# Chunks 3 to 7 of a DeltaNet and PReLU block: the first pair by seven products too, odd steps with keys ahead of rows

## The chip, the cores and the metric

The kernel runs on one core of a Trainium2 chip. The time of a run is the device time of that core in microseconds; less is better. Engines are named as the profile names them: PE is TensorE (PEld its loads of weights), DVE is VectorE, ACT is ScalarE, POOL is GpSimd, SP is SyncE, whose queue issues nearly all transfers.

## The reference

Two blocks run one after the other. The first is DeltaNet attention (4 batches, 8 heads, 768 tokens, head dimension 48), a recurrence over a 48 x 48 state for each head. The second turns its output into 3072 rows of 384 numbers and sends them through two matrices with a PReLU between them. Everything is 32-bit floating point.

```
k_n = k / (norm(k) + 1e-6);  state = 0
for t in range(768):                                    # for each batch and head
    y[t]  = q[t] @ state
    v_old = k_n[t] @ state
    state = state + beta[t] * outer(k_n[t], v[t] - v_old)
x = y as (3072, 384)
h = x @ w_in                                            # w_in: 384 x 2048
g = max(h, 0) + alpha * min(h, 0)                       # alpha: one slope per column
out = g @ w_out                                         # w_out: 2048 x 384
```

## The kernel before

**Steps and chunks.** The sequence is cut into 12 chunks of 64 tokens. A step is one chunk for two of the four batches (`steps`, L115), so step n belongs to chunk n // 2, and there are 24. The attention of a step is solved by blocks: keys and queries are transposed on PE (`flips`, L478), Gram products of the keys are made nine steps ahead (`grams`, L513), a triangular system is inverted for four steps at once on DVE (`eliminate`, L588: 30 multiplications and additions at L602 and L608, and transposes at L577), and the state is used and updated (`through_state`, L838, `solve`, L951, `outputs`, L963, `next_state`, L977).

**The feed-forward part.** Once both steps of a chunk are through, their 256 rows go through the two matrices. `to_ffn` (L999) transposes the outputs y of a step on PE (L1006), and ACT copies them from PSUM into the tile `xt` of the chunk (L1010). The 2048 columns of the first matrix are 8 pairs of 128-column blocks. A *plain* pair (`plain`, L1316) is six matmuls of 128 x 256 (L1321), a Relu on ACT (L1326) and two operations on DVE (L1328). In chunks 3 to 11 most pairs are instead done by a scheme of seven products over four quarter blocks (`pair`, L1335): four *shared* products of 128 columns into a bank of PSUM (`common`, L1370, matmul at L1357), which ACT copies out (L1376) and POOL combines by three additions (L1381), and three *own* ones (`own`, L1359, matmuls at L1347 and L1352), with the third block of 128 rows done plainly. Its *total* is one DVE operation (L1385), then come a Relu on ACT (L1391), in chunks 3 to 7 two scalings on ACT (L1394), and the *slope*, one operation on DVE (L1398). The scheme needs sums of blocks of `w_in`, which POOL makes once (`input_sums`, L1257), and sums of blocks of `xt`, which DVE makes for each chunk (`token_sums`, L1292, four operations at L1303). The second matrix follows in seven products (`ffn_out_faster`, L1456, matmuls at L1481, additions at L1477).

**Pairs before the change.** In chunks 3 to 7 pairs 1 to 6 (`QUICK`, L1228) are done by seven products and pairs 0 and 7 are plain (L1431 and L1438); from chunk 8 on all eight are by seven products.

**PSUM.** From step 8 on there are two double tiles `p_pair` for attention and four banks for the feed-forward part, two named `p_ffn` and two `p_more`. The two double tiles are handed out in turn (`ps_big`, L78). A bank can be written again when its last reader is done.

**Order.** The order on each engine is written out by hand: engines run their instructions in program order. The feed-forward part is a generator (`feed_forward`, L2061) that yields 76 parts a chunk, 48 for the first matrix and 28 for the second, and `weave` (L1529) deals its parts between the other work. A step n from 8 on has three stretches (loop at L2102). First `burst_a(n)` (L1575): outputs and state update of step n - 1, then the state product of step n. Then `turn_round(n)` (L1617): the rows of step n - 1 and the flips of later keys and queries. Then `burst_b(n)` (L1601): the solve of step n, Gram products, queries and products for the steps after. `FILL` and `FILLS` (L2099, L2100) say how many parts of the feed-forward part go into each of the three stretches, and `TURNS` and `PIECES_OF` (L2098, L2094) how many pieces of the elimination go with them. What a burst leaves for later (`later`) is spread over the stretch. Within the first matrix, `Due` (L1271) issues a pair's total, Relu and slope so many parts after its start.

Of the kernel before, what the change touches and what calls it, by code (L numbers as in the profile page):

```python
# [25 lines left out]
FP32 = mybir.dt.float32  # L26
# [13 lines left out]
ASK = 8  # L40
# [5 lines left out]
def kernel(  # L46
# [340 lines left out]
        two("a_t", [128, H, C]), two("r", [128, 2, G, D]), two("u", [128, 2, G, D])  # L387
    )

    def one_of(tiles, n):  # L390
        return tiles[n % 2 if n < ONE else 0]

# [26 lines left out]
        stats[n] = (first_norm[:, n], first_weight[:, n])  # L419

    def squared(n):
        ksq[n] = work.tile([128, H, D], FP32, name="ksq", bufs=2)
        nc.scalar.square(ksq[n], early(n)[:, :, 0:D])

    def norms(n):
# [11 lines left out]
    def weigh(n):  # L437
        if n >= N:
            return []
        norm = stats[n]  # L440
        root(norm)
        return [lambda: weigh_rest(n, norm)]
# [782 lines left out]
        yield  # L1225

    held = {}
    QUICK = range(1, FP - 1)  # L1228
    beyond_sums = sums[:, FP // 2 : FP]
    late_pads = [x.rearrange("p h d -> p (h d)") for x in (k_late[0], masks_[1])]  # L1230

    def spare(x):

        if not held:
            held["same"] = work.tile([128, NJ, H, HB], FP32, name="same", bufs=1)
        return held["same"].rearrange("p j h c -> p (j h c)")[:, x * 256 : x * 256 + 256]

    def units_of(tile_):
        names = " ".join("abc"[: len(tile_.shape) - 1])
        return tile_.rearrange(f"p {names} -> p ({names})").rearrange("p (i e) -> p i e", e=128)  # L1240

    def group_sums(which, x):

        if which == 0:
            return units_of((k_early[0], k_early[2], q_pad[1])[x])
        if which == 3:
            return spare(x).rearrange("p (i e) -> p i e", e=128)
        return units_of((rights_, solved_)[which - 1][1])[:, x : x + 1]

    GROUPS = [slice(1, 5), slice(5, 6), slice(6, 7), slice(0, FP, FP - 1)]  # L1250

    def input_sum(x, i):

        which = 3 if i in (0, FP - 1) else max(i - 4, 0)
        return group_sums(which, x)[:, i - 1 if which == 0 else i // 7]

    def input_sums(which):  # L1257

# [48 lines left out]
    def ffn_in_fast(c):  # L1307
# [103 lines left out]
        def run(gen):  # L1411
            for _ in gen:
                due.step()
                yield

        if some:
            for at in (44, 47, 55, 60):
                due.put(at, lambda: next(first, None))
            for at in (52, 53, 57, 62):
                due.put(at, lambda: next(rest, None))  # L1420
            own_banks = [ffn_banks[(BANK + i) % 3] for i in (0, 1)]
            q_banks, three_z = [ffn_banks[3], ffn_banks[(BANK + 2) % 3]], [sums[:, 0 : FP // 2, 2], *two_z]
            pairs = {
                i: pair(i, own_banks[i % 2], q_banks[i % 2], three_z[i % 3]) for i in QUICK
            }
            for i, (_, _, total, below, slope) in pairs.items():
                late = i - (FP - 2)
                due.put(PER * i + (9 if late < 0 else 7), total)
                due.put(PER * i + {0: 10, -1: 12}.get(late, 13), below)
                due.put(PER * i + {0: 12, -1: 16}.get(late, 17), slope)  # L1430
            yield from plain(0, own_banks[0])  # L1431
            for i in QUICK:
                if i == QUICK[0]:
                    yield from run(pairs[i][1]())
                if i + 1 in QUICK:
                    yield from run(pairs[i + 1][1]())
                yield from run(pairs[i][0]())
            yield from plain(FP - 1, q_banks[(FP - 1) % 2])  # L1438
            return

        due.put(PER * 6 + 5, lambda: next(first, None))
# [14 lines left out]
    def ffn_out_faster(c):  # L1456
# [53 lines left out]
        if last:  # L1510
            store(c, 0, o[0], left)
        yield from some(p[6], sum_(2), weight(1, 1), range(FP - 2))
        if c + 1 < NCH:
            assert c + 1 in whole
            token_sums(c + 1)
        yield from some(p[6], sum_(2), weight(1, 1), range(FP - 2, FP))
        add(o[0][:, right_], o[0][:, right_], p[6])
        store(c, 0, o[0], right_ if last else slice(0, DM))
# [97 lines left out]

    def turn_round(n):  # L1617

        if n > JOINED:
            to_ffn(n - 1)  # L1620
        flips(n + EARLY + 1, n + 2)
        later = weigh(n + EARLY + 1)
        load_next(n)
        load_q(n + 3)
        return later
# [434 lines left out]

    def feed_forward():  # L2061
        yield from ffn_in(2)
        for which in range(3):
            input_sums(which)
        for i, _ in enumerate(ffn_out_fast(2)):
            if i == FAST_PARTS - 2:
                assert SOME in whole
                token_sums(SOME)
            yield
        for c in range(SOME, NCH):  # L2070
            yield from ffn_in_fast(c)
            if c == ALL - 1:
                input_sums(3)
            yield from ffn_out_faster(c)

    tail = feed_forward()
# [8 lines left out]
    for n in range(NJ, JOINED):  # L2085
# [95 lines left out]
```

## Time and profile before

| | |
|---|---|
| median of 3 runs | 646.55 us (646.39 to 647.15) |
| the profiled execution | 646.92 us |
| span of its profile | 645.2 us |
| busy, PE / DVE / ACT / POOL | 628.4 / 502.8 / 300.0 / 192.3 us |
| start of the plain pair 0 of chunks 3 to 7 | 219.15, 270.41, 320.31, 371.07 and 419.43 us |
| granted TensorE clock | 0.996 of full speed |

The span is what the profiler sees between the first and the last instruction; the run's time is 1.7 us longer. In the page and in the answers of the trace, a group of instructions is given with its line in the kernel, its engine, operation, tiles and shape. A matmul of 32-bit numbers is recorded as two instructions, so x12 stands for six. Matmuls overlap, so the time of one is read from the distance between the starts of its neighbours and not from its own length. "Idle before" names what an engine last waited for.

### The profile page before, as it was taken

What the parts mean: (1) busy time and instruction counts of PE and PEld (TensorE: products, weight loads), DVE (VectorE), ACT (ScalarE), POOL (GpSimd) and SP (SyncE); (2) the same over time, 40 slices, a digit from 0 to 9 for tenths busy, and PEclk for the clock granted to TensorE, in tenths of its full rate; (3) what the DMA queues carried; (4) which work ended last, traced back from release to release, by engine and by line L of the source; (5) the groups of instructions that cost most, each with busy time, mean ns of one, the idle gap of its engine ahead of it and who ended that gap; (6) DMA issues with size and microseconds to landing.
All of it is one profiled execution on the core that took longest, in us unless ns stands there. A gap on an engine that the chain in (4) does not pass through costs nothing.

```text
span 645.2 us, 22078 instructions
## 1 busy us (share of the span) xinstructions
PE 628.4 (97%) x9357; PEld 561.9 (87%) x9357; DVE 502.8 (78%) x1182; ACT 300.0 (47%) x695; POOL 192.3 (30%) x358
## 2 busy tenths in 40 slices
PE   7899999999999989999999999999999999999997
PEld 6687777566889989999989989999999999999997
DVE  5868789978997889868969958969968478377383
ACT  6676654254553276177177267057055054041230
POOL 7267610010161051052041043044053053062350
PEclk9989999999999999999999999999999999999999
DMA  7756864113301311311312111111211210100000
GB/s 130 202 157 174 240 150 117 28 24 69 71 18 24 76 33 20 70 30 28 60 30 39 35 40 28 36 42 26 46 34 25 54 24 1 42 11 2 26 1 24
DMA packets 106802, 36.92 MB, mean 57 GB/s; under 512 B 99872, under 2 KB 103088, under 8 KB 106704
## 3 DMA queue, kind: packets, MB, share of 16 engines
q1 hardware_dynamic: 104832, 35.03, 24.6%
q8 instruction: 73, 1.20, 0.8%
q10 hardware_dynamic: 1872, 0.49, 0.4%
q14 instruction: 25, 0.20, 0.1%
HBM read 30.78 MB, written 4.72 MB: 55 GB/s over the span
## 4 chain that ended last, share of the span: by engine, by line
PE 77%; DVE 12%; ACT 4%; DMA 3%; issue 2%; POOL 1%; SPq 0%; DVEq 0%; POOLq 0%; ACTq 0%
PE p_more L1481 15%; PE p_ffn L1481 11%; PE p_more L1357 5%; PE p_ffn L1155 5%; PE p_ffn L1347 4%; PE p_more L1347 3%; PE p_ffn L1112 3%; PE p_ffn L1352 3%; PE p_ffn L1177 3%; PE p_more L1352 3%; PE p_pair L784 2%; PE p_pair L467 2%; PE p_ffn L1321 2%; PE p_more L1321 2%; PE p_pair L844 2%
## 5 line engine op out<-in xcount | busy, mean ns | idle before, releaser
L1381 POOL TENSOR_TENSOR sums<-sums 128x128 f32<-128x128 f32 x186 | 109.7, 593 | 206.0 <-ACT sums L1376 196.3
L1112 PE MATMUL p_ffn<-xt,w_in 128*128 128x256 f32 x288 | 69.7, 388 | 1.2 <-DVE act L1124 0.8
L1112 PEld LDWEIGHTS p_ffn<-xt,w_in 128*128 128x128 f32 x288 | 52.1, 190 | 10.1 <-ACT w_out L267 0.7
L1010 ACT COPY xt<-p_pair 128x384 f32<-128x384 f32 x22 | 10.4, 478 | 105.0 <-PE p_pair L1006 96.0
L608 DVE TENSOR_TENSOR block<-block,prod 128x30 f32<-128x30 f32 (+9 forms) x150 | 51.7, 345 | 5.1
L602 DVE TENSOR_TENSOR prod<-block 128x30 f32<-128x30 f32 (+9 forms) x150 | 52.0, 346 | 4.3 <-POOL block L592 2.7
L456 POOL TENSOR_TENSOR beta_t<-beta_t,rec 128x8 f32<-128x8 f32 x20 | 5.7, 287 | 164.2 <-DVE rec L450 157.8
L1481 PE MATMUL p_more<-w_out,act 128*128 128x192 f32 x288 | 52.1, 329 | 0.0
L1481 PEld LDWEIGHTS p_more<-w_out,act 128*128 128x128 f32 x288 | 47.0, 190 | 0.4
L1376 ACT COPY sums<-p_more 128x512 f32<-128x512 f32 x43 | 25.1, 583 | 40.5 <-PE p_more L1357 34.1
L1347 PE MATMUL p_ffn<-xt,w_in 128*128 128x256 f32 x140 | 41.8, 381 | 0.0
L1385 DVE TENSOR_TENSOR act<-p_ffn,sums 128x512 f32<-128x512 f32 x35 | 23.8, 679 | 15.2 <-POOL sums L1381 10.8
L1347 PE MATMUL p_more<-xt,w_in 128*128 128x256 f32 x108 | 32.8, 385 | 0.0
L796 ACT COPY inv<-p_pair 32x256 f32<-32x256 f32 x40 | 14.4, 361 | 27.2 <-DVE u L958 26.4
L1481 PE MATMUL p_ffn<-w_out,act 128*128 128x192 f32 x144 | 26.3, 326 | 0.0
L1391 ACT ACTIVATE a_t<-act 128x512 f32<-128x512 f32 x31 | 19.5, 630 | 14.1 <-DVE act L1385 14.1
L1481 PE MATMUL p_more<-w_out,sums 128*128 128x192 f32 x144 | 24.9, 326 | 0.0
L1401 DVE SCALAR_TENSOR_TENSOR act<-a_t,al_t,act 128x256 f32<-128x256 f32 x32 | 20.5, 680 | 5.5 <-ACT a_t L1391 5.4
L1385 DVE TENSOR_TENSOR act<-p_more,sums 128x512 f32<-128x512 f32 x27 | 18.5, 684 | 7.9 <-POOL sums L1381 5.7
L1481 PEld LDWEIGHTS p_ffn<-w_out,act 128*128 128x128 f32 x144 | 23.9, 190 | 0.0
L1481 PEld LDWEIGHTS p_more<-w_out,sums 128*128 128x128 f32 x144 | 23.2, 190 | 0.0
L958 DVE TENSOR_TENSOR u<-p_pair,wgt 128x384 f32<-128x384 f32 x20 | 11.1, 552 | 15.5 <-PE p_pair L784 15.5
(324 smaller groups left out, 1682.2 us busy)
## 6 DMA issues: line engine op xcount, KB each, us to landing
v_raw<-in_v_dram SPq DMA_DIRECT2D x48, 96.0 KB, 2.9
qp<-in_q_dram SPq DMA_DIRECT2D x48, 96.0 KB, 2.9
out_dram<-o_sb SPq DMA_DIRECT2D x90, 48.0 KB, 1.6
space_out<-in_moe_w_out_dram SPq DMA_DIRECT2D x11, 384.0 KB, 4.6
ke<-in_k_dram SPq DMA_DIRECT2D x43, 96.0 KB, 3.3
kl<-in_k_dram SPq DMA_DIRECT2D x80, 48.0 KB, 2.4
w_out<-in_moe_w_in_dram SPq DMA_DIRECT2D x6, 512.0 KB, 4.8
w_out<-in_moe_w_out_dram SPq DMA_DIRECT2D x5, 384.0 KB, 3.7
```

What stands on the lines that cost most here:

```text
L602: nc.vector.tensor_tensor(out=prod, in0=r[:, 0:j, j : j + 1].to_broadcast([128, j, n]), in1=r[:, j : j + 1, j + 1 : HB].to_broadcast([128, ...
L608: nc.vector.tensor_tensor(out=r[:, 0:j, j + 1 : HB], in0=r[:, 0:j, j + 1 : HB], in1=prod, op=ALU.add)
L1112: nc.tensor.matmul(p_h[:, i], w_in[:, t, (f + i) * 128 : (f + i + 1) * 128], xt[:, t], start=(t == 0), stop=(t == KT - 1),)
L1155: nc.tensor.matmul(p_o[u], gs[f // 2][:, f % 2, u * 128 : (u + 1) * 128], w_out[:, f], start=(f == 0), stop=(f == FT - 1),)
L1321: nc.tensor.matmul(p[:, f], w_in[:, k, j * 128 : j * 128 + 128], xt[:, k], start=(k == 0), stop=(k == KT - 1),)
L1347: nc.tensor.matmul(p[:, f * 256 : f * 256 + 256], w(2, f), xt[:, 2], start=True, stop=False)
L1352: nc.tensor.matmul(p[:, j * 128 : j * 128 + 128], a, b, start=False, stop=(j > 0))
L1357: nc.tensor.matmul(q[:, j], a, b, start=True, stop=True)
L1376: nc.scalar.copy(z, q)
L1381: nc.gpsimd.tensor_tensor(out=dst, in0=a, in1=b, op=ALU.add)
L1385: nc.vector.tensor_tensor(out=g.rearrange("p f (u e) -> p (f u) e", u=2), in0=p.rearrange("p (i e) -> p i e", e=128), in1=z, op=ALU.add,)
L1481: nc.tensor.matmul(p, x(i), w(i), start=(i == 0), stop=(i == FP - 1))
```

## The change

In chunks 3 to 7, pair 0 is done by seven products as well; only pair 7 stays plain. The shared products of pair 0 are the first instructions of the chunk, then come its own, the shared ones of pair 1, those of pair 2, the own ones of pair 1, and so on. The banks of the shared products swap their parity. The sums of `w_in` for pair 0 are made with those of pairs 1 to 3 before chunk 3, pairs 4, 5 and 6 each get a group of their own, and the last group, made after chunk 7's first matrix, holds pair 7 alone. For room, the two tiles of squares (`ksq`) become fixed ones; from step 16 on only one of them is used.

In `turn_round`, steps from 9 on with an odd number flip keys and queries first and issue the transposes of rows later, as the last of what the stretch spreads out. Steps with an even number issue the token sums of the coming chunk right after the rows, and not in the last product of the chunk before; those of the last chunk are issued after the last rows.

`FILLS` deals 12, 12 and 10 parts to the stretches of an even step (before 12, 10, 12), and `TURNS` and `PIECES_OF` deal the pieces of the elimination anew.

```diff
+    squares_ = two("ksq", [128, H, D])
 ...
     def squared(n):
-        ksq[n] = work.tile([128, H, D], FP32, name="ksq", bufs=2)
+        ksq[n] = squares_[n % 2 if n < LONE - 1 else 0]
 ...
-    QUICK = range(1, FP - 1)
+    QUICK = range(FP - 1)
 ...
-    GROUPS = [slice(1, 5), slice(5, 6), slice(6, 7), slice(0, FP, FP - 1)]
+    GROUPS = [slice(0, 4), *(slice(i, i + 1) for i in range(4, FP))]
 ...
             pairs = {
-                i: pair(i, own_banks[i % 2], q_banks[i % 2], three_z[i % 3]) for i in QUICK
+                i: pair(i, own_banks[i % 2], q_banks[(i + 1) % 2], three_z[i % 3]) for i in QUICK
             }
 ...
-            yield from plain(0, own_banks[0])
-            for i in QUICK:
-                if i == QUICK[0]:
-                    yield from run(pairs[i][1]())
+            yield from run(pairs[0][1]())
+            yield from run(pairs[0][0]())
+            yield from run(pairs[1][1]())
+            for i in QUICK[1:]:
                 if i + 1 in QUICK:
                     yield from run(pairs[i + 1][1]())
                 yield from run(pairs[i][0]())
-            yield from plain(FP - 1, q_banks[(FP - 1) % 2])
+            yield from plain(FP - 1, q_banks[1])
 ...
         yield from some(p[6], sum_(2), weight(1, 1), range(FP - 2))
-        if c + 1 < NCH:
-            assert c + 1 in whole
-            token_sums(c + 1)
 ...
     def turn_round(n):
-        if n > JOINED:
+        after = n > ASK and n % 2 == 1
+        if n > JOINED and not after:
             to_ffn(n - 1)
+            if n >= 2 * SOME + 2:
+                token_sums(n // 2 - 1)
         flips(n + EARLY + 1, n + 2)
         later = weigh(n + EARLY + 1)
+        if after:
+            later.append(lambda: to_ffn(n - 1))
         load_next(n)
         load_q(n + 3)
         return later
 ...
-        JOINED + 1: (0, 4, 7), JOINED + 2: (4, 4, 4),
+        JOINED + 1: (0, 4, 7), JOINED + 2: (4, 5, 4),
     }
-    TURNS = [(6, 2, 2), (2, 2, 7), (7, 2, 2), (0, 3, 8)]
-    FILL = {JOINED: (8, 12, 12), JOINED + 1: (10, 12, 10), JOINED + 2: (8, 10, 12)}
-    FILLS = [(12, 10, 12), (12, 18, 12)]
+    TURNS = [(5, 3, 2), (2, 3, 6), (5, 3, 3), (0, 4, 7)]
+    FILL = {JOINED: (8, 12, 12), JOINED + 1: (10, 12, 10), JOINED + 2: (8, 12, 10)}
+    FILLS = [(12, 12, 10), (12, 18, 12)]
 ...
     stretch(12, iter(()), 0, burst_a(N))
     to_ffn(N - 1)
+    token_sums(NCH - 1)
```

More of the change, by code (lines that the diff above doesn't have):

```diff
@@ L1235, in spare @@
             held["same"] = work.tile([128, NJ, H, HB], FP32, name="same", bufs=1)
-        return held["same"].rearrange("p j h c -> p (j h c)")[:, x * 256 : x * 256 + 256]
+        return held["same"].rearrange("p j h c -> p (j h c)")[:, x * 128 : x * 128 + 128]
     def units_of(tile_):
@@ L1245, in group_sums @@
             return units_of((k_early[0], k_early[2], q_pad[1])[x])
-        if which == 3:
+        if which == 4:
             return spare(x).rearrange("p (i e) -> p i e", e=128)
-        return units_of((rights_, solved_)[which - 1][1])[:, x : x + 1]
-    GROUPS = [slice(1, 5), slice(5, 6), slice(6, 7), slice(0, FP, FP - 1)]
+        return units_of((rights_, solved_, squares_)[which - 1][1])[:, x : x + 1]
+    GROUPS = [slice(0, 4), *(slice(i, i + 1) for i in range(4, FP))]
     def input_sum(x, i):
-        which = 3 if i in (0, FP - 1) else max(i - 4, 0)
-        return group_sums(which, x)[:, i - 1 if which == 0 else i // 7]
+        return group_sums(max(i - 3, 0), x)[:, i if i < 4 else 0]
     def input_sums(which):
@@ L1512, in ffn_out_faster @@
         yield from some(p[6], sum_(2), weight(1, 1), range(FP - 2))
-        if c + 1 < NCH:
-            assert c + 1 in whole
-            token_sums(c + 1)
+        assert c + 1 == NCH or c + 1 in whole
         yield from some(p[6], sum_(2), weight(1, 1), range(FP - 2, FP))
@@ L2062, in feed_forward @@
         yield from ffn_in(2)
-        for which in range(3):
+        for which in range(4):
             input_sums(which)
[L2065 to L2069, printed above, removed]
+        yield from ffn_out_fast(2)
         for c in range(SOME, NCH):
@@ L2072, in feed_forward @@
             if c == ALL - 1:
-                input_sums(3)
+                input_sums(4)
             yield from ffn_out_faster(c)
```

## The prediction

> **What bounds the kernel now.** I read four views in this order: the page's busy table, the stretches of chunks 3 to 7 (one row per chunk, the sixth row the first chunk that the change leaves alone), the waits of TensorE in that region, and then the timelines of PE, DVE and ACT around those waits. "Own" and "shared" are the two groups of products of a pair, S the start of a chunk.
>
> ```profile
> PE 628.4 (97%) x9357; PEld 561.9 (87%) x9357; DVE 502.8 (78%) x1182; ACT 300.0 (47%) x695; POOL 192.3 (30%) x358
> ```
>
> PE is busy 97% of the span, so a gain has to come out of PE's own work or out of its few waits.
>
> ```profile
> 219.15:270.41 51.26, 49.58 (x780) 46.51 (x779) 45.06 (x106) 26.11 (x62) 11.66 (x22) 1.00 0.21 40
> 270.41:320.31 49.90, 49.57 (x779) 46.51 (x779) 39.47 (x93) 26.92 (x64) 13.59 (x24) 1.00 0.21 42
> 320.31:371.07 50.76, 49.57 (x779) 46.50 (x779) 42.92 (x103) 26.31 (x62) 11.75 (x22) 1.00 0.21 40
> 371.07:419.43 48.36, 48.02 (x740) 45.19 (x739) 38.49 (x91) 23.60 (x54) 12.53 (x22) 1.00 0.18 35
> 419.43:466.80 47.37, 47.37 (x707) 44.62 (x707) 40.73 (x91) 22.18 (x50) 14.63 (x22) 1.00 0.17 35
> 466.80:515.00 48.20, 48.20 (x727) 46.20 (x726) 33.15 (x63) 18.51 (x42) 13.95 (x24) 1.00 0.19 39
> ```
>
> Columns are length, then busy time of PE, PEld, DVE, ACT and POOL. Length less PE is 1.68, 0.33, 1.19, 0.34 and 0.00 us: 3.54 us of waiting, all in chunks 3 to 6. At chunk 7 and later there is nothing to remove but work. The granted clock is 1.00 throughout. The waits have two names:
>
> ```profile
> PE p_pair L467 <- DVE a_t L545: 2.2, 2, 1.3
> PE p_ffn L1357 <- ACT sums L1376: 1.3, 4, 0.3
> ```
>
> The first (1.35 us in chunk 3, 0.85 in chunk 5) is an odd step's flip of the next keys waiting until DVE has masked the matrix in the same PSUM tile. The second (0.33 us in each of chunks 3 to 6) is the shared products of pair 3 waiting for the copy of pair 1 out of their bank.
>
> ```profile
> 276.15 0.39 PE L1357 MATMUL p_more<-xt,w_in 128*128 128x128 f32 x2
> ...
> 277.05 0.60 PE L1347 MATMUL p_ffn<-xt,w_in 128*128 128x256 f32 x2
> ...
> 290.70 0.60 PE L1347 MATMUL p_ffn<-xt,w_in 128*128 128x256 f32 x2
> ...
> 292.24 0.60 PE L1347 MATMUL p_more<-xt,w_in 128*128 128x256 f32 x2
> ...
> 293.77 2.76 PE L1321 MATMUL p_ffn<-xt,w_in 128*128 128x256 f32 x12
> 296.46 0.68 PE L954 MATMUL p_pair<-r,inv 64*64 64x48 f32 x32
> ```
>
> The timeline of chunk 4 on PE (start, length, line, operation). Starts give the prices: own products 292.24 - 290.70 = 1.54 us, a plain pair 296.46 - 293.77 = 2.69, shared products 277.05 - 276.15 = 0.90.
>
> **The change, part by part.** (1) *Pair 0 by seven products.* 0.90 + 1.54 = 2.44 for 2.69 us on PE: -0.25 a chunk, -1.25 us in five, all on the path. Nine loads of weights replace six; the columns fall from 1536 to 1408, and the 128-column products already run back to back at 0.22 us in the rows above, so I add nothing for loads. ACT loses a Relu from PSUM (0.59) and gains a copy (0.58), a Relu (0.63) and two scalings (0.50 each): +1.6 us a chunk. The first 26 us of chunk 4 have ACT busy 18.45 us; 20.1 still fits. DVE loses two operations (0.87 together) and gains a total (0.68) and a slope (0.68): about +0.5 us. POOL gains three additions, 1.87 us a chunk.
>
> (2) *The shared products of pairs 0 and 1 now stand ahead of the second burst of attention.* Pair 3's bank is then copied out long before it is wanted: -0.33 in four chunks, -1.3 us. Late next would be the plain pair 7, whose bank is now pair 6's: it needs that copy. Before, the copy ended at 292.70 and the plain pair began at 293.77, 1.07 us of slack. ACT has 1.6 us more to do, less the 0.48 us copy of rows that now comes after it and less its idle waits of 0.88 and 0.85 us earlier in that chunk. I take 0 to 0.3 us a chunk, 0.3 in all.
>
> (3) *Odd steps: keys flipped ahead of rows.* The flip then takes the PSUM tile that DVE's state update left (its last reader at 285.15 in chunk 4, well ahead of the flip at 288.24), and not the one that the mask holds: -2.2 us. The rows go into the masked tile in the middle of plain pair 7, some 6 us later, so the wait does not move with them. The next Gram products need the copy of the rows out of that tile; it stands on ACT between the slopes of pairs 5 and 6, about 0.6 us ahead of need. Nothing on SP moves: the two orders of its transfers are the same.
>
> (4) *Token sums right after an even step's rows.* On DVE they pass the two additions that empty the bank of the fifth product, the one that pair 0's shared products want. In chunk 4 the queue then ends its additions near 269.0 against S = 270.25: no wait. In chunk 5 DVE is behind: its multiplication of 238 ends at 318.98 before; sums 1.0 and additions 0.6 follow, less the two small steps (0.87) that the new dealing does earlier: 319.7 against 320.14, less what PE gained. I take 0.2 (0 to 0.5). Chunk 7 is 0.6 us better off: 0. Chunk 3 is different: the last product of chunk 2 ends in the very bank that pair 0 wants, so PE stands for DVE's addition (0.35) and its hand-overs: +0.45, once. The store behind those additions goes out up to 1 us later; nothing waits for it.
>
> (5) *Chunk 3's DVE.* Between 219 and 240.2, the end of the total of pair 3, DVE idled 0.37 + 0.73 + 1.91 = 3.0 us; afterwards only about 1.2 us (the wait for the solve) is left, since totals no longer wait for POOL. Against these 1.8 us stand one elimination step more (0.85) and +0.4 of pair 0: total 3 ends near 239.7. Own products of pair 5, which need it, began at 240.81. So chunk 3 gains about 1.1 us, start wait included, and not the 1.93 of its three terms (0.25 + 0.33 + 1.35). In chunk 5 DVE idled 1.19 + 0.73 + 2.81 us in the same part, and the full 0.25 + 0.33 + 0.85 is there.
>
> (6) *POOL beside DVE.* With POOL at work, DVE's operations stretch:
>
> ```profile
> 336.64 1.22 DVE L1398 TENSOR_TENSOR act<-act,a_t 128x512 f32<-128x512 f32 x1
> ...
> 338.86 0.89 DVE L602 TENSOR_TENSOR prod<-block 128x220 f32<-128x220 f32 x1
> ...
> 340.69 0.68 DVE L1398 TENSOR_TENSOR act<-act,kl 128x512 f32<-128x512 f32 x1
> ```
>
> The first is 0.54 us over the third; the second 0.51 over 0.38 for the same shape at 315.12. All such excess of chunk 5 (also 0.31, 0.14, 0.25 and 0.13) is 1.9 us for its 18 additions, 0.1 each. Fifteen more make 1.5 us of DVE, 0.3 a chunk, on the path only where DVE is full: +0.3 in chunk 3, +0.1 in chunk 5. The Trainium skill, SBUF — State Buffer, section "Who interferes with whom", says that a VectorE instruction with two inputs in SBUF and a GpSimd instruction that reads SBUF exclude each other for the whole instruction. The trace agrees in kind (0.68 becomes 1.22); by the rule at its worst each added addition would cost DVE its whole length, which the second rival works out from rows.
>
> (7) *The rest at nothing.* Four more input sums before chunk 3 (0.46 to 0.90 us each) fall into POOL's idle 7.9 us before 198.12; uncovered they cost 2.3. One square buffer from step 16 on: one use a step. Chunks 8 to 11 have no PE wait now and only rows and sums moved: 0, at most 0.3 either way.
>
> **Sum.** Chunk 3 -1.1 + 0.3; chunk 4 -0.58; chunk 5 -1.43 + 0.2 + 0.1; chunk 6 -0.58; chunk 7 -0.25; copies +0.3: -3.0 us. The profiled execution took 646.92 us (span 645.2 and 1.7 around it), 0.37 over the median of 646.55; it gives 643.9, and against the median 643.5, which I predict.
>
> **The rivals.** *A: only the work goes.* The waits come back under other names: chunk 5's and 7's openings wait for the additions as chunk 3's does (0.45 each), pair 7 and the Gram products for ACT in four chunks (0.3 to 0.4 each). That eats some 2.3 us: 645.3 to 646.4. For it speaks DVE's 45.06 of 51.26 us in chunk 3; against it the 2.8 us that DVE idles for POOL in chunk 5, which early totals free.
>
> *B: POOL's fifteen extra additions hold DVE up in full, and DVE holds PE's banks.* 5 x 1.87 = 9.4 us of DVE on the path for the 0.4 charged: 643.5 + 9.0 = 652.5. It decides the sign from 0.87 us a chunk on (3.0 + 1.3 over five). For it speaks the 1.22 us row; against it the 0.1 us that an addition costs on average, and that a total reads PSUM and stays at 0.67 to 0.69 in all its rows.
>
> *C: all waits go and none comes,* -1.25 - 3.54: 641.8.
>
> **How the numbers follow.** Forecast (642.0 to 645.2) 0.63, A 0.20, B and anything else slower 0.13, C 0.04. No change is 0.2%, 1.3 us, about what this kernel's measurement can tell: 645.26 to 647.84. A lies mostly inside, 0.03 of it outside. Faster 0.70, same 0.17, slower 0.13. The range 642.0 to 646.3 leaves out B, C and A's edge; where both signs are held, the forecast's own range is 642.0 to 645.2.
>
> **What would show it.** The flip of odd steps without a wait on the mask; pair 3's shared products without one on the copy; about 0.45 us on the first product of chunk 3, and less than 0.5 on that of chunk 5; PE's busy time of a chunk down by about 0.25; total 3 of chunk 3 ending some 20.5 us after the chunk's start. Wrong it would be if PE waits on DVE totals in the middle of chunks 3 to 6, if the plain pair 7 waits for ACT, or if slopes on DVE lengthen to 1 us and more throughout.

## The result, and the profile after

The changed kernel is slower: 658.5 us, median of four runs (657.07 to 658.88), against 646.55 us (646.39 to 647.15) of the kernel before. The ratio is 1.0179 (1.0161 to 1.0197). In a later comparison beside 29 runs of the kernel before on one chip (median 648.81, 646.51 to 651.57) it was 1.0147 (1.0119 to 1.0176). Between two profiled executions of one kernel the difference lies before chunk 3, as shown further down, so most of what follows compares chunks 3 to 7 of the profiled executions.

The page of the changed kernel, busy time of the engines:

```profile
PE 634.2 (97%) x9387; PEld 567.4 (86%) x9387; DVE 502.4 (76%) x1182; ACT 306.0 (47%) x710; POOL 201.3 (31%) x377
```

TensorE has 30 recorded matmul instructions more, that is 15 matmuls, and its busy time rose by 5.8 us, stretches of half clock among it, where a small fall was forecast. The stretches of chunks 3 to 7 of the changed kernel show where (length, then busy PE, PEld, DVE, ACT, POOL, and the granted clock; a chunk's opening wait is in its length):

```profile
222.49:276.91 54.42, 50.88 (x785) 48.26 (x786) 47.32 (x107) 27.50 (x65) 13.72 (x25) 0.97 0.20 39
276.91:329.07 52.16, 49.62 (x785) 46.62 (x784) 40.17 (x95) 28.17 (x67) 14.68 (x27) 1.00 0.21 40
329.07:381.78 52.71, 49.54 (x785) 46.86 (x785) 42.42 (x100) 27.60 (x65) 13.33 (x25) 1.00 0.19 38
381.78:431.33 49.55, 48.09 (x746) 45.35 (x745) 38.51 (x91) 24.62 (x57) 15.11 (x25) 1.00 0.17 34
431.33:478.63 47.30, 47.30 (x713) 44.97 (x713) 40.77 (x91) 23.43 (x53) 14.40 (x25) 1.00 0.17 35
```

Together 256.14 us against 247.65: 8.5 us more. Length less busy PE is 10.71 us of waiting, where 3.54 stood before (+7.2). Chunk 3 also has a granted clock of 0.97 and 50.88 us of work, 1.5 more than the same products take at full clock in a later run (49.36). The work itself hardly moved. Of the 12.0 us between the two profiled spans, the other 3.5 lie before chunk 3.

The waits of TensorE in chunks 3 to 7 of the changed kernel (total, times, longest):

```profile
PE p_more L1348 <- DVE act L1386: 6.5, 4, 3.0
PE p_ffn L1348 <- DVE act L1386: 2.2, 2, 1.2
PE p_pair L786 <- issue: 1.1, 1, 1.1
PE p_ffn L1358 <- DVE o_sb L1199: 0.5, 1, 0.5
PE p_ffn L1358 <- DVE o_sb L1478: 0.3, 1, 0.3
```

Both old names are gone, as forecast. In their place own products (L1348) wait 8.7 us for totals on VectorE (L1386) to empty their bank. The worst wait, in chunk 3's timeline on PE:

```profile
242.13 1.22 PE L1348 MATMUL p_more<-xt,w_in 128*128 128x256 f32 x2 [3.01 <-DVE act L1386]
```

Why that total was late stands in VectorE's timeline of the same chunk (total 1, the reduction of the squares, the scaling of the values, total 2):

```profile
232.23 0.68 DVE L1386 TENSOR_TENSOR act<-p_ffn,sums 128x512 f32<-128x512 f32 x1
...
236.30 0.55 DVE L432 TENSOR_REDUCE norm<-ksq 128x8 f32<-128x384 f32 x1 [2.31 <-ACT ksq L425]
...
238.52 1.08 DVE L823 TENSOR_TENSOR v_raw<-v_raw,norm 128x384 f32<-128x384 f32 x1
...
241.39 0.68 DVE L1386 TENSOR_TENSOR act<-p_more,sums 128x512 f32<-128x512 f32 x1
```

VectorE stands idle for 2.31 us ahead of the reduction, until ScalarE has squared the keys; everything behind it, total 2 among it, waits along. ScalarE's timeline shows what the square stood behind:

```profile
232.92 0.62 ACT L1392 ACTIVATE kl<-act 128x512 f32<-128x512 f32 x1
233.58 0.91 ACT L1395 ACTIVATE kl<-kl,al_t 128x256 f32<-128x256 f32 x2
234.50 0.82 ACT L570 COPY same<-right 32x256 f32<-32x256 f32 x2
235.33 0.40 ACT L773 COPY wgt<-wgt 64x4 f32<-64x4 f32 x2
235.75 0.52 ACT L425 ACTIVATE ksq<-ke 128x384 f32<-128x384 f32 x1
```

The first two are pair 0's Relu and scalings, which the change added: 1.5 us. In chunk 5 the same reduction waited 3.31 us; in chunks 3 to 6 such waits come to 7.3 us, against 0.9 before.

The same place in the kernel before (total 1, the reduction, total 2; the chunk starts at 219.0):

```profile
229.67 0.69 DVE L1385 TENSOR_TENSOR act<-p_ffn,sums 128x512 f32<-128x512 f32 x1 [1.91 <-POOL sums L1381]
...
230.47 0.55 DVE L430 TENSOR_REDUCE norm<-ksq 128x8 f32<-128x384 f32 x1
...
234.76 0.68 DVE L1385 TENSOR_TENSOR act<-p_more,sums 128x512 f32<-128x512 f32 x1
```

There VectorE waited 1.91 us for GpSimd ahead of total 1, and by then the square was all but done. In the changed kernel total 1 no longer waits, as forecast, but the reduction behind it does. Total 2 starts 18.9 us after the chunk's start and not 15.8.

Last, the stretches around that 3 us wait (columns as above: behind POOL stands the granted clock, then the DMA share and GB/s):

```profile
238.00:242.04 4.04, 1.13 (x11) 0.94 (x9) 3.96 (x8) 0.69 (x2) 3.01 (x5) 1.00 0.08 16
242.04:245.45 3.41, 3.32 (x13) 3.13 (x14) 3.30 (x8) 2.00 (x4) 1.07 (x3) 0.50 0.02 5
245.45:249.00 3.55, 3.55 (x27) 3.37 (x26) 2.89 (x6) 3.15 (x8) 0.59 (x1) 1.00 0.72 131
```

The clock reads 1.00, 0.50, 1.00: behind the wait TensorE had half its clock for 3.41 us, with 13 recorded matmul instructions where the next stretch has 27. The wait cost 3.0 us and its echo 1.5.

### The profile page after: what moved, and what is told of

It is laid out like the page before. It is cut to its first block, busy times and chain, and to the rows that moved or that the text cites. A ratio compares the mean times of both kernels' runs of the same rounds, so it can differ in the third digit from the quotient of the medians.

```text
span 657.2 us, 22184 instructions
## 1 busy us (share of the span) xinstructions
PE 634.2 (97%) x9387; PEld 567.4 (86%) x9387; DVE 502.4 (76%) x1182; ACT 306.0 (47%) x710; POOL 201.3 (31%) x377
## 4 chain that ended last, share of the span: by engine, by line
PE 64%; DVE 17%; issue 7%; ACT 6%; POOL 3%; DMA 2%; SPq 0%; DVEq 0%; POOLq 0%; ACTq 0%
PE p_more L1482 11%; PE p_ffn L1482 8%; PE p_ffn L1157 5%; PE p_more L1358 5%; PE p_ffn L1114 4%; PE p_ffn L1348 3%; PE p_more L1348 3%; PE p_ffn L1179 3%; PE p_ffn L1353 2%; PE p_more L1353 2%; PE p_pair L786 2%; PE p_pair L469 2%; DVE prod L604 2%; DVE block L610 2%; PE p_ffn L1358 2%
## 5 line engine op out<-in xcount | busy, mean ns | idle before, releaser
L1382 POOL TENSOR_TENSOR sums<-sums 128x128 f32<-128x128 f32 (+1 forms) x201 | 119.4, 596 | 300.9 <-ACT sums L1377 290.1
L1114 PE MATMUL p_ffn<-xt,w_in 128*128 128x256 f32 x288 | 71.1, 394 | 2.1 <-ACT act L1124 1.2
L610 DVE TENSOR_TENSOR block<-block,prod 128x30 f32<-128x30 f32 (+9 forms) x150 | 53.2, 355 | 5.2
L1348 PE MATMUL p_more<-xt,w_in 128*128 128x256 f32 x128 | 39.7, 392 | 6.5 <-DVE act L1386 6.5
L1348 PE MATMUL p_ffn<-xt,w_in 128*128 128x256 f32 x140 | 42.3, 384 | 2.2 <-DVE act L1386 2.2
L1377 ACT COPY sums<-p_ffn 128x512 f32<-128x512 f32 x24 | 13.9, 577 | 33.5 <-PE p_ffn L1358 30.4
L1392 ACT ACTIVATE kl<-act 128x512 f32<-128x512 f32 x36 | 22.7, 629 | 12.4 <-DVE act L1386 12.3
L1386 DVE TENSOR_TENSOR act<-p_ffn,sums 128x512 f32<-128x512 f32 x35 | 23.8, 680 | 5.2 <-PE p_ffn L1353 2.8
L1392 ACT ACTIVATE a_t<-act 128x512 f32<-128x512 f32 x31 | 19.6, 631 | 16.0 <-DVE act L1386 15.7
L1348 PEld LDWEIGHTS p_more<-xt,w_in 128*128 128x128 f32 x128 | 19.8, 193 | 8.0 <-DVE act L1386 7.3
L1386 DVE TENSOR_TENSOR act<-p_more,sums 128x512 f32<-128x512 f32 x32 | 21.8, 681 | 5.2 <-POOL sums L1382 5.2
```

Of the source, the lines that this page charges most:

```text
L610: nc.vector.tensor_tensor(out=r[:, 0:j, j + 1 : HB], in0=r[:, 0:j, j + 1 : HB], in1=prod, op=ALU.add)
L1114: nc.tensor.matmul(p_h[:, i], w_in[:, t, (f + i) * 128 : (f + i + 1) * 128], xt[:, t], start=(t == 0), stop=(t == KT - 1),)
L1348: nc.tensor.matmul(p[:, f * 256 : f * 256 + 256], w(2, f), xt[:, 2], start=True, stop=False)
L1377: nc.scalar.copy(z, q)
L1382: nc.gpsimd.tensor_tensor(out=dst, in0=a, in1=b, op=ALU.add)
L1386: nc.vector.tensor_tensor(out=g.rearrange("p f (u e) -> p (f u) e", u=2), in0=p.rearrange("p (i e) -> p i e", e=128), in1=z, op=ALU.add,)
```

## The experiments

Four theories were set against each other. Theory 1: pair 0's new ScalarE work delays the square, the square holds the head of VectorE's queue, and totals come late. Theory 2: GpSimd's fifteen additions hold VectorE up (the prediction's second rival). Theory 3: the new dealing of elimination pieces puts too much ahead of the totals. Theory 4: the start-up is dearer because the square tiles have a new place. "Middle" is chunks 3 to 7 in the profiled execution, with the opening wait of chunk 3: 247.65 us before, 256.1 after. Times are medians, ratios are to the kernel before on the same chip.

**The square first.**

```diff
 def burst_b(n):
...
+    if n + EARLY + 2 < N:
+        squared(n + EARLY + 2)
     soon = solve(n, b[:, :, 0:WY])
...
-    return gram[2:] + [lambda: squares(n + EARLY + 2)]
+    return gram[2:] + [lambda: n + EARLY + 2 < N and norms(n + EARLY + 2)]
```

> The changed kernel with one move on ScalarE: the square of the next keys is issued first in the second half of each step, ahead of pair 0's Relu and scalings; its reduction on VectorE stays where it was. Theory 1 (the reduction of the squares waits for ScalarE at the head of VectorE's queue, and the totals that PE wants stand behind it): the reduction's waits fall from 7.3 us in chunks 3 to 6 to under 1.5, PE's waits on totals from 8.7 to under 2.5 us, the clock drop of chunk 3 goes with them (1.7 us), and the time falls from 658.5 to 649-651. Theory 2 (GpSimd's fifteen extra additions hold VectorE up) and theory 3 (the new dealing of elimination pieces overfills VectorE): nothing they name is changed, so 657-659. Start-up (theory 4: the new place of the square tiles costs 3.5 us before chunk 3): chunk 3 still starts near 222.5.

Measured: 650.96 us, ratio 1.0022 (0.9999 to 1.0046), middle 249.3. In VectorE's timeline of chunk 3 of this run the reduction no longer waits, and total 2 starts 15.7 us after the chunk's start at 220.75 and not 18.9:

```profile
232.19 0.54 DVE L432 TENSOR_REDUCE norm<-ksq 128x8 f32<-128x384 f32 x1
...
236.48 0.68 DVE L1386 TENSOR_TENSOR act<-p_more,sums 128x512 f32<-128x512 f32 x1
```

PE's waits for totals fall from 8.7 to 3.9 us and the clock stays at 1.00 through the middle. One place in one engine's order, and nothing else, gave back 6.8 of 8.5 us: theory 1 holds. But 3.9 is more than its 2.5, so it isn't alone.

**The dealing of before.**

```diff
-    JOINED + 1: (0, 4, 7), JOINED + 2: (4, 5, 4),
+    JOINED + 1: (0, 4, 7), JOINED + 2: (4, 4, 4),
-TURNS = [(5, 3, 2), (2, 3, 6), (5, 3, 3), (0, 4, 7)]
+TURNS = [(6, 2, 2), (2, 2, 7), (7, 2, 2), (0, 3, 8)]
...
-FILLS = [(12, 12, 10), (12, 18, 12)]
+FILLS = [(12, 10, 12), (12, 18, 12)]
```

(and the last entry of FILL in the same way)

> The changed kernel with the dealing of elimination pieces and the fills of before. Theory 3 (the dealing): the waits on totals go and the time falls to about 650. Theory 1: the reduction of the squares still stands behind pair 0's ScalarE work; one elimination step fewer ahead of total 1 to 3 may save 0.5 to 1 us in a chunk, and the time stays within 656 to 659.5. Theory 2: unchanged, 657-659.

Measured: 652.39 us, 1.0055 (1.0034 to 1.0076), middle 251.5. The 650 of theory 3 and the 656 of theory 1 both missed: waits for totals 3.8 us here. The reduction still waits, 4.0 us in sum, but fewer pieces stand ahead of the totals. Pair 3's shared products wait 0.34 us for the copy again in chunks 3 to 5, since the fills went with the dealing. Theory 3 holds as a second cause of about the same waits, with the reserve that this run changes turns and fills at once; the turns alone are moved further down.

**Pair 0 alone,** with odd steps, token sums and dealing of before.

```diff
-        after = n > ASK and n % 2 == 1
-        if n > JOINED and not after:
+        if n > JOINED:
             to_ffn(n - 1)
-            if n >= 2 * SOME + 2:
-                token_sums(n // 2 - 1)
...
```

(and the dealing as in the last run)

> The kernel before with pair 0 by seven products (order of the products, banks, input sums and square tiles as changed), but with the steps, token sums and dealing of before. Theory 1: pair 0's Relu and scalings alone delay the square, so VectorE's reduction waits 2 us or more in chunks 3 and 5 and PE waits on totals: 653-659. If the loss comes from the reordered odd steps or the dealing instead: 644-646, plus 3.5 if the start-up is dearer with the moved square tiles.

Measured: 656.09 us, 1.0095 (1.0064 to 1.0126), middle 255.5. From the waits in its PE timeline, chunk 3:

```profile
239.59 0.70 PE L1348 MATMUL p_more<-xt,w_in 128*128 128x256 f32 x2 [1.99 <-DVE act L1386]
...
242.40 1.10 PE L469 MATMUL p_pair<-ident,ke 128*112 128x128 f32 x4 [1.34 <-DVE a_t L547]
```

The late total and the old wait for the mask stand one behind the other, and 6.83 us of half clock begin during the second (241.28 to 248.11): 56.7 us for the chunk, opening wait included, the longest of all runs. Pair 0 by itself brings a middle 7.9 us longer than before, of the change's 8.5, though some 2.9 us of it (half of 5.7 us of busy PE) are this long stretch of half clock.

**The odd steps alone,** in the kernel before.

```diff
+        after = n > ASK and n % 2 == 1
-        if n > JOINED:
+        if n > JOINED and not after:
             to_ffn(n - 1)
         flips(n + EARLY + 1, n + 2)
         later = weigh(n + EARLY + 1)
+        if after:
+            later.append(lambda: to_ffn(n - 1))
```

> The kernel before with the odd steps' keys flipped ahead of the rows, and nothing else. By the step of the prediction: the two waits of the flip on the mask (2.2 us) go and no other comes: 644.2-644.8. If the waits move (the next user of the tile waits): 646-647. The start-up is instruction by instruction that of before: chunk 3 starts near 219.0, clock 1.00 from 10 to 22 us.

Measured: 648.59 us beside 648.81, ratio 0.9993 (0.997 to 1.0016), middle 247.2: nothing but 0.5 us. The flips wait no more, but in chunk 3

```profile
242.65 0.70 PE L1347 MATMUL p_ffn<-xt,w_in 128*128 128x256 f32 x2 [1.22 <-DVE act L1385]
```

and 0.59 us in chunk 5 likewise (own products of pair 5, total 3). Total 3 is done 21.3 us after the chunk's start, as before (240.3 - 219.0): VectorE set the date, and TensorE only came earlier to wait for it.

**Square first and the dealing of before together.**

```diff
-    JOINED + 1: (0, 4, 7), JOINED + 2: (4, 5, 4),
+    JOINED + 1: (0, 4, 7), JOINED + 2: (4, 4, 4),
...
+    if n + EARLY + 2 < N:
+        squared(n + EARLY + 2)
...
```

(both edits above, whole)

> The changed kernel with both moves at once: the squares first on ScalarE, and the dealing and fills of before. Theory 1 and 3 together (each of them alone gave back about half of PE's waits on totals: 8.7 us became 3.9 in either, because both lengthen the same VectorE queue ahead of totals 1 to 3): under 1.5 us of waits on totals in chunks 3 to 6, no clock drop in chunk 3, chunk 3 at 50 to 50.7 us, chunks 3 to 7 together 245 to 247 (before 247.6, changed 255.6). If a third cause is behind the rest, waits on totals stay over 2.5 us.

Measured: 650.08 us, 1.0023 (1.0004 to 1.0041), middle 248.4. Missed: 2.55 us of waits for totals remain (0.48 and 1.25 in chunk 3, 0.82 in chunk 5), the last two of them on total 3, as with the odd steps alone.

**The same with rows ahead of keys.**

```diff
-        after = n > ASK and n % 2 == 1
-        if n > JOINED and not after:
+        if n > JOINED:
             to_ffn(n - 1)
-            if n >= 2 * SOME + 2:
+            if n % 2 == 0 and n >= 2 * SOME + 2:
                 token_sums(n // 2 - 1)
         flips(n + EARLY + 1, n + 2)
         later = weigh(n + EARLY + 1)
-        if after:
-            later.append(lambda: to_ffn(n - 1))
```

> As the squares-first kernel with the old dealing, but odd steps put the rows ahead of the keys again, so the flips wait for the mask once more. If VectorE sets the pace of chunks 3 and 5 and the flip's wait only takes the place of a wait on totals (as in the run with the odd steps alone, where 1.8 of 2.2 us came back): within 0.8 us of that kernel over chunks 3 to 7. If the flip's 2.2 us are PE's own loss: 2 us and more longer.

Measured: 650.14 us, 1.003 (1.001 to 1.005), middle 249.2, that is 0.8 more. The flips wait 1.34 and 1.18 us for the mask, and total 3 is then no longer waited for: as long as VectorE sets the date of total 3, the exchange of keys and rows changes little more than the name of the wait.

**GpSimd's work alone,** added to the kernel before.

```diff
...
+            for dst, a, b in (
+                (idle_[:, 0], idle_[:, 0], idle_[:, 1]), (idle_[:, 1], idle_[:, 0], idle_[:, 1]),
+                (idle_, idle_, idle_),
+            ):
+                due.put(8, lambda dst=dst, a=a, b=b: nc.gpsimd.tensor_tensor(out=dst, in0=a, in1=b, op=ALU.add))
             yield from plain(0, own_banks[0])
```

> The kernel before with three more GpSimd additions in each of chunks 3 to 7 (two of 128x128, one of 128x256, on a tile of their own, fifteen in all as in the change) and nothing else. Theory 2 (GpSimd's additions hold VectorE up for their whole length, 1.9 us a chunk): chunks 3 and 5 1.5 us longer or more, 3 to 9 us in all. Theory 1: at most 0.5 us a chunk, from totals that wait for GpSimd's other additions, chunks 3 to 7 within 247.6 to 249.

Measured: 649.3 us, 1.0009 (0.9992 to 1.0025), middle 248.7: 0.53, 0.29 and 0.19 us in chunks 3 to 5, nothing in 6 and 7. Theory 2 falls: 1.0 us for fifteen additions that took 8.0 us, not 9. The changed kernel itself agrees: in chunks 3 to 7 VectorE has 484 operations as before and is busy 209.2 us against 206.7, and these 2.5 us are what pair 0's longer total and slope come to (0.5 a chunk).

**ScalarE's work alone,** added to the kernel before.

```diff
...
+            for _ in range(3):
+                due.put(10, lambda: nc.scalar.mul(idle_, idle_, al_t[:, 0:1]))
             yield from plain(0, own_banks[0])
```

> The kernel before with three ScalarE operations on a tile of their own (128x256 each, 1.5 us) in each of chunks 3 to 7, at the place where pair 0's Relu and scalings stand in the changed kernel, and nothing else. Theory 1: the reduction of the squares waits for ScalarE (0.9 us before, now 3 or more in chunks 3 to 6), totals 1 and 2 come late and chunks 3 to 6 are 0.5 to 2 us longer each where VectorE is full (3 and 5), 2 to 5 us in all. If ScalarE's extra work is hidden: within 0.5 us of before.

Measured: 654.15 us, 1.0081 (1.0052 to 1.0111), middle 253.4. Its VectorE timeline, chunk 3, has the changed kernel's wait (L433 is here the reduction, L426 the square):

```profile
233.83 0.55 DVE L433 TENSOR_REDUCE norm<-ksq 128x8 f32<-128x384 f32 x1 [1.60 <-ACT ksq L426]
```

Such waits come to 5.5 us in chunks 3 to 6, against 0.9. 1.6 us a chunk on an engine that is 47% busy cost 5.7 us in the middle. This is theory 1's beginning without any of the rest: no seven products, no dealing, no odd steps. Here TensorE meets the delay mostly as longer waits for the mask, which also stands behind the reduction on VectorE (3.9 us, 2.2 before), and as 1.3 us of waits for totals. In chunk 5 a wait of 1.91 us was again followed by 3.41 us of half clock.

**The changed kernel once more,** without an edit.

> The changed kernel once more, for its start-up and its middle. If the 3.5 us before chunk 3 belong to the change (the square tiles' place), chunk 3 starts beyond 222 again and the half-clock stretches of the first 50 us last over 10 us; if they differ from run to run, it starts anywhere between 219 and 223. The middle is to come out as it was: 3 us of wait at pair 4 of chunk 3, a clock drop behind it, chunks 3 to 7 at 255.6 within 0.5.

Measured: 658.15 us; the middle is 256.4 with the same waits to 0.2 us, so the middle is the program's. The start-up isn't: chunk 3 starts at 220.4 us, not 222.5. The half-clock stretches of the first 50 us, first the one of the kernel before, then the two of the changed kernel as first profiled, then the two of this run:

```profile
32.86:36.28 3.42, 3.24 (x120) 3.08 (x112) 2.03 (x7) 1.05 (x2) 1.78 (x2) 0.50 0.30 67
```

```profile
13.35:20.18 6.83, 6.39 (x79) 4.83 (x78) 5.96 (x19) 5.03 (x16) 3.30 (x8) 0.50 0.97 192
...
37.24:44.07 6.83, 6.83 (x95) 5.08 (x88) 3.56 (x7) 4.78 (x9) 2.56 (x4) 0.50 0.66 151
```

```profile
12.55:15.96 3.41, 2.70 (x13) 2.73 (x14) 3.06 (x8) 2.65 (x10) 2.98 (x9) 0.50 0.70 121
...
36.45:39.86 3.41, 3.41 (x70) 2.68 (x68) 1.82 (x4) 2.04 (x5) 1.32 (x2) 0.50 0.64 126
```

3.4, 13.7 and 6.8 us of half clock. The run with the odd steps alone has the start-up of before, instruction by instruction, and had 6.83 us of it and chunk 3 at 221.3. Over all profiles but that of the last run below, chunk 3 starts at 218.4 to 221.3 us with the old square tiles (six, median 220.0) and at 219.8 to 222.5 with the new ones (nine, median 220.6). Two executions of one start-up thus differ by 2 us and more, and the medians by 0.6: theory 4's 3.5 us fall, and only a small cost of the new place stays possible.

**The rest of the queue's order.** The square first, and two turns dealt so that a piece less stands ahead of total 3 in chunks 3 and 5:

```diff
-TURNS = [(5, 3, 2), (2, 3, 6), (5, 3, 3), (0, 4, 7)]
+TURNS = [(5, 3, 2), (1, 4, 6), (7, 2, 2), (0, 4, 7)]
```

> The squares-first kernel with two turns of the dealing altered: one elimination piece moved behind the third total of the odd step in chunks 3 and 5 (turn 2,3,6 becomes 1,4,6), and the even step ahead of chunk 4 dealt as before (7,2,2). If the rest of the loss is the order of VectorE's queue ahead of totals 2 and 3 (1.36, 0.86 and 1.37 us of waits left in the squares-first run): these three fall under 0.4 each and chunks 3 to 7 take 245 to 246 (squares first 248.8, before 247.65). If VectorE is simply full, the waits stay over 2.5 us in sum.

Measured: 647.69 us, 0.9979 (0.9963 to 0.9996), middle 245.5. The three waits are 0.26, 0.23 and 0.18 us, and no other wait for totals is left:

```profile
PE p_ffn L1348 <- DVE act L1386: 0.4, 2, 0.3
PE p_more L1348 <- DVE act L1386: 0.2, 1, 0.2
```

VectorE wasn't full; its order was wrong.

**The re-dealt kernel with rows ahead of keys,** by the same edit of the odd steps as before.

```diff
-        if n > JOINED and not after:
+        if n > JOINED:
             to_ffn(n - 1)
...
```

> The same kernel with rows ahead of keys in odd steps again. Now that totals are early, the flip's wait for the mask should be PE's own loss: 2 us or more longer over chunks 3 to 7 than with keys first. If it is worth nothing even here, within 0.8 us.

Measured: 651.58 us, 1.0045 (1.0026 to 1.0065), middle 250.1: 4.6 us longer. The flips wait for the mask four times, longer than in the kernel before:

```profile
PE p_pair L469 <- DVE a_t L547: 4.7, 4, 1.8
```

The same exchange of keys and rows was worth 0.5 us in the kernel before and is worth 4.6 here, where totals cost 0.2 us and the whole wait is TensorE's own.

**The odd steps and one turn,** in the kernel before, pair 0 plain.

```diff
-TURNS = [(6, 2, 2), (2, 2, 7), (7, 2, 2), (0, 3, 8)]
+TURNS = [(6, 2, 2), (1, 3, 7), (7, 2, 2), (0, 3, 8)]
```

(and the odd steps as in the run with these alone)

> The kernel before with keys first in odd steps and one elimination piece moved behind total 3 there (turn 2,2,7 becomes 1,3,7); pair 0 stays plain. If the waits that took the flips' place (1.22 and 0.59 us) are of the queue's order, they go: chunks 3 to 7 at 245.0 to 245.8, and the time 1.5 to 2.5 us under before. If VectorE is full: 247 as with the odd steps alone.

Measured: 645.96 us, 0.9956 (0.994 to 0.9972), middle 245.0. The 1.8 us of the run with the odd steps alone are gone; only the copies' four waits of 0.34 remain.

**And the changed kernel's fills,** pair 0 still plain.

```diff
-FILLS = [(12, 10, 12), (12, 18, 12)]
+FILLS = [(12, 12, 10), (12, 18, 12)]
```

(and the last entry of FILL in the same way)

> The kernel with odd steps' keys first and one elimination piece behind total 3, and now also the changed kernel's fills (12,12,10), which put the second burst behind pair 1's shared products; pair 0 stays plain. If the fills free pair 3's shared products of their 0.34 us wait as in the changed kernel: chunks 3 to 7 at 243.4 to 244.4 (245.0 without the fills), the time 0.5 to 1 us under that kernel's. Pair 0 by seven products (chunks 3 to 7 at 244.9 and 0.54 of start wait in the re-dealt kernel) is then worth nothing here. If the wait stays or a total becomes late: 245 or more.

Measured: 645.18 us, 0.9953 (0.9934 to 0.9971); its interval and the last run's overlap. The stretches of its chunks 3 to 7:

```profile
219.18:269.24 50.06, 49.63 (x781) 46.79 (x780) 45.13 (x108) 26.23 (x62) 11.94 (x22) 1.00 0.22 42
269.24:318.80 49.56, 49.36 (x779) 46.63 (x779) 39.74 (x95) 26.66 (x64) 13.01 (x24) 1.00 0.22 42
318.80:368.12 49.32, 49.32 (x780) 46.63 (x779) 41.73 (x101) 26.32 (x62) 11.66 (x22) 1.00 0.22 41
368.12:415.88 47.76, 47.76 (x741) 45.23 (x740) 38.25 (x91) 23.50 (x54) 13.34 (x22) 1.00 0.18 35
415.88:463.17 47.29, 47.29 (x708) 44.76 (x708) 40.33 (x91) 21.98 (x50) 15.04 (x22) 1.00 0.18 35
```

Middle 243.99, with 0.6 us of waiting left (two totals, 0.43 and 0.20). This beats the kernel before by half a per cent and the changed one by more, with the change's odd steps and fills, one turn dealt otherwise, and without seven products for pair 0. The reduction waits for the square in this kernel too, 1.77 us in chunk 3 and 1.84 in chunk 5, yet the first costs TensorE at most the 0.43 us and the second nothing. A wait of VectorE costs only what it adds to the end of an operation that TensorE stands for.

**The gap of chunk 6.** Seven us into chunk 6 every kernel with pair 0 by seven products has a gap on TensorE that no wait explains: 0.3 to 1.5 us, 1.14 in the changed kernel, always behind the 5941st recorded matmul instruction, at whichever line that is. None with pair 0 plain has it.

```diff
     identities(6, big[1][:, 0])
+    short(200, big[1][:, 0])
```

(in the re-dealt kernel with the square first)

> The re-dealt squares-first kernel with 200 tiny matmuls (32x32, identities) more at the very start, ahead of all work, and nothing else. If the gap of chunk 6 (1.45 us at the 5941st matmul) belongs to the count in TensorE's stream, it leaves the elimination products of chunk 6: chunk 6 falls from 49.3 to about 48.0 and a gap, if any, shows 200 matmuls earlier in the work, in chunk 5's outputs or chunk 6's opening. If it belongs to that place of the work, chunk 6 stays at 49.3. The start-up may be up to 3 us longer.

Measured: 667.56 us, 1.0273 (1.0246 to 1.03); the tiny matmuls lengthened the start-up by over 20 us, far more than expected. Chunk 6 falls from 49.28 to 47.77, as the count would have it. The waits of its PE timeline in the middle now include

```profile
348.93 0.38 PE L1358 MATMUL p_ffn<-xt,w_in 128*128 128x128 f32 x1 [1.17 <-issue]
...
372.12 1.41 PE L1482 MATMUL p_more<-w_out,act 128*128 128x192 f32 x7 [0.38 <-issue]
```

The second stands behind the 5943rd recorded instruction, now in chunk 5's outputs; the first is new, behind the 5560th, seven us into chunk 5, just behind the elimination products as in chunk 6 before. So the place of the work doesn't carry the gap; where the stream of instructions stands does. The traces also list transfers of the kind "instruction", 16 KB each. One of them lands shortly before each of the eleven gaps ends, and TensorE goes on 1.34 to 1.56 us after the landing: in the changed kernel it runs from 386.18 to 387.06, and the gap from 387.47 to 388.62. In the kernel before the transfer of that place lands at 376.19, when TensorE has left the tiny elimination products (64 recorded instructions in 0.56 us) and is in longer ones, and it never stops. So instructions that arrive late fit every gap and the kernel that is spared; that they are the cause is inferred from these times, since no run moved the transfer alone.

## Why the prediction was wrong

It gave 643.5 us, faster with 0.70, and the kernel is 9 to 12 us slower, above every rival it named. By its own steps:

*Step 1, pair 0.* ScalarE's addition was sized rightly at 1.6 us a chunk, and then dismissed: 18.45 of 26 us busy (the trace has 18.24), so "20.1 still fits". This is the sentence that failed. A sum of busy time says whether an engine can do the work, not when each piece gets done. The added pieces stand ahead of the square of the next keys, the reduction of that square stands on VectorE ahead of total 1 or 2, and the square's slack in the kernel before was nil, as its reduction in chunk 4 shows:

```profile
281.45 0.56 DVE L430 TENSOR_REDUCE norm<-ksq 128x8 f32<-128x384 f32 x1 [0.88 <-ACT ksq L423]
```

Two runs show it from both sides: the added work without the rest costs 5.7 us, and moving the square ahead in the whole change wins back 6.8 of the 8.5 that it lost. The gain on TensorE was also too large. A plain pair of 2.69 us had been taken from a row ahead of products of another shape; where the next products are of the same shape it takes 2.59 (269.24 to 271.83 in the last kernel), and seven products 2.43 (271.56 to 273.99 in the re-dealt one): 0.16 and not 0.25. Over five chunks these two kernels differ by 0.55 us of busy PE (243.36 and 242.81), and the gap of chunk 6 and the opening of chunk 3 take more than that back. In the changed kernel itself no fall shows: chunks 4 to 7 have 194.55 us of busy PE against 194.53 before.

*Step 2, the shared products first,* was right: none of the 0.33 us waits is left, and plain pair 7 never waits.

*Step 3, keys ahead of rows.* The waits on the mask went, as said, but the 2.2 us weren't to be had for that alone: only 0.5 came in the kernel before. "The wait does not move with them" failed; it moved to total 3, the next thing on VectorE that TensorE wants.

*Step 4, the openings,* was right: 0.54 (0.45 forecast) and 0.34 (0.2).

*Step 5, VectorE in chunk 3.* Total 3 was to end 20.5 to 20.7 us after the chunk's start; it ended at 24.4. Busy pieces and remaining idle time had been added up, with 1.2 us of idle time for the solve and none for the square. VectorE idled 2.98 us ahead of total 3 (0.67 for the solve, 2.31 for the square), as much as the 3.0 before: the 1.9 us of waiting for GpSimd went, and the square's took their place. And 11 elimination steps start between the chunk's start and total 3 where 9 did, two more and not one. With the square first and one piece moved behind it, TensorE starts the products that need total 3 at 20.3 us: the working was right for a queue without that wait, and that queue also needs another dealing than the change's. What matters of a piece is on which side of a total it stands.

*Step 6, GpSimd beside VectorE:* 0.4 us charged, 1.0 measured; the rival that made it 9.4 is dismissed by the run.

*Step 7.* Chunks 8 to 11 are untouched, as said (178.5 us from chunk 8 to the end, 178.6 before), and for the start-up nothing beyond what one execution differs from the next by is seen.

*Not in any step:* half a clock behind long waits, 1.5 us in chunk 3, and the gap of chunk 6, 1.14 us.

The prediction named its own refutation: PE waiting on VectorE's totals in the middle of chunks 3 to 6. No rival gave that a mechanism except GpSimd's additions. The third form, ScalarE's new work ahead of something that VectorE waits for, was one row away: the wait of the reduction for the square, in the kernel before.

## What to carry to other kernels

When work goes to an engine with room, don't ask whether the sum fits; list what stands behind the new pieces in that engine's order, who waits for the first of those, and what stands behind that waiter on its own engine. A wait that is taken off the bound engine is only worth the time until the next date that another engine sets, so look for that date (here: total 3 ends 21.3 us after the chunk's start) before counting the gain. And an unrelated instruction that can run early, like the square here, belongs ahead of new work and not behind it.

## What the runs showed of the hardware that was not expected

The granted clock is either 1.00 or 0.50, and 0.50 lasts 3.41 us or twice that. In chunks 3 to 7 it fell behind single waits of TensorE of 1.91, 1.99 (twice) and 3.0 us (twice), and not where two waits of 1.6 and 1.2 stood 5 us apart. But the length of a wait doesn't decide alone. The run with GpSimd's work had a wait of 1.67 us that ended at 70.97 us and one of 1.88 that ended at 241.19; the clock fell behind the first alone:

```profile
69.08:72.49 3.41, 1.74 (x68) 1.44 (x67) 3.20 (x10) 2.45 (x5) 2.98 (x5) 1.00 0.52 103
72.49:75.90 3.41, 3.41 (x12) 2.65 (x11) 2.63 (x8) 1.69 (x3) 2.09 (x2) 0.50 0.61 191
239.74:243.15 3.41, 1.96 (x16) 1.91 (x17) 3.33 (x7) 1.20 (x3) 1.74 (x3) 1.00 0.26 50
```

The recorded clock changes on a grid of 3.41 us, and the 1.88 us straddle two of its stretches. Between 60 and 600 us of all sixteen profiles, every stretch of the grid in which TensorE was idle for 1.67 us or more (six, up to 2.91) is followed by half clock, and none with 1.60 or less is; in the first 60 us less was enough at times. A wait of about 2 us can therefore be dearer here than its length. The Trainium skill, TensorE: Matmul & The Clock Gate, section "Part 1: The HAM clock gate (the "warmup" mystery)", gives the same two rates and a free-running window of 3413 ns, and says that the phase makes the start of a kernel vary from run to run; the traces agree (stretches of 3.41 and 6.83 us; 3.4 and 6.8 us of half clock in two start-ups of the same instructions, 13.7 and 6.8 in two of the changed kernel). It puts the fall at one idle window of about 3.4 us; here about half of such a window idle was enough.

Fifteen additions on GpSimd, 8.0 us of its time, cost the middle 1.0 us. And TensorE's gaps behind a fixed number of recorded instructions, up to 1.5 us, each ending about 1.45 us after a 16 KB transfer of instructions has landed, are a cost that a reordering can bring or lose without any wait of the program's own.
